# Attention: value products of two chunks in every second step, hash signs by one operation and small transfers

## Chip, cores and metric

One core of one Trainium2 chip runs the whole program. The metric is the device time of one execution in microseconds. The kernel before takes 656.63 us, the median of three runs (654.44 to 657.75).

## What is computed

Three parts follow each other: an attention with hashed masks, and two mixture-of-experts layers. The change lies in the attention, but for one reordering at the end of the last layer. Cut to what matters:

```python
def _attn_ref(q, k, v, proj):              # q, k, v: 2 x 8 heads x 768 x 64, proj: 64 x 6
    q_bits = (einsum('bhsd,dk->bhsk', q, proj) > 0)
    k_bits = (einsum('bhsd,dk->bhsk', k, proj) > 0)
    q_bucket, k_bucket = sum(bits * 2 ** arange(6), axis=-1)     # for each of the two
    mask = q_bucket[:, :, :, None] == k_bucket[:, :, None, :]
    scores = where(mask, scale * q @ k.T, -1e9)
    attn = softmax(scores)                  # with 1e-9 added to the sum
    return attn @ v
```

Two layers follow, `_moe_ref` (routing by capacity, 8 experts of 512 x 1024 x 512) and `_moe2_ref` (a gate per token, one expert per token). All inputs and outputs are float32.

## The kernel before

The attention works on 16 units. A unit `u` is a pair of heads (a = 0, 1) and one half (384 rows) of the queries; it has six steps `i`, each for one head and 128 queries, so 96 steps in all. A step written in the loop of `attention` issues, in this order:

- `score(u, i)`: four matmuls into the PSUM tile S (L191, the product of the rounded parts Q1 and K1, and L193, that of Q2 and K2, each of 512 and 256 columns). Rows 64 to 75 of Q2 and K2 hold the twelve sign rows of the hash, so the mask comes out of L193. VectorE then takes the negated maximum (L195) and two small operations (L196, L197) that give the scale g and the bias b of the exponential. S has two buffers, so the S of a step needs the exponential of two steps before to be done.
- the splits of Q and K for later units (L130, L139, L146), and the loads (L113, L117, L124) on the queue of SyncE (SP), all in program order.
- `av(u', c)`: the product of the transposed probabilities PT with the values, for one of six chunks `c` of 128 keys. One call issues a matmul for each head (L227), each in its own half of the array's columns. Steps 4 and 5 of a unit do chunks 0 and 1 of the unit before, steps 0 to 3 chunks 2 to 5 of the unit before that one.
- `project(...)`: the hash projections of the next unit's queries (step 3), and of keys (step 3, and in some units step 1). Up to four matmuls (L162), each with 64 rows and 12 columns of weights in its own corner of the array, write rows 0 to 11 of the four quarters of one PSUM tile `aux`. VectorE then makes a sign tile of each (L168 for queries, L176 for keys), writing straight to rows 64 to 75 of Q2 or K2. Two of these follow in the step of the projection, the others in the next step.
- `tpose(u', ip, cp)`: four transposes (L213) into one PSUM tile pT (two buffers) and its copy by ScalarE to PT (L216). An even step does two of these groups, an odd step one.
- `expo(u, i)`: the exponential on ScalarE (L204), with the sum of the row. In an even step it lies between the two copies of PT on ScalarE, in an odd step behind the one copy.

At step 0, `fin` (L270) turns a finished unit to rows, and the router's logits come of it. The order on each engine is the order in which the program issues: nothing reorders it. TensorE changes between three ways of being divided: whole (S, transposes, `fin`), two column halves (`av`), and eight corners (`project`).

`splits` and `projs` (set up before the loop) say at which step each split and projection comes; `kplan` says at which unit which key block is split and projected. Units 5 to 8 take two key blocks each; the second is projected at step 1 of the next unit. Keys come through three buffers (`kd`), which are free again when split and projected. `later`, at step 3 of unit 2, issues the constants of the two later layers, among them a chain of small GpSimd operations and three SP transfers behind it (L1103, L1107).

In the last layer, `tile2` computes a tile of 128 tokens; its result `o` (L1441), two small operations on the row index (`ix`, `ixi`, L1444 and L1446) and the scatter by GpSimd (L1454) end it.

Of the kernel before, what the change touches and what calls it, by code (L numbers as in the profile page):

```python
# [7 lines left out]
F32 = mybir.dt.float32  # L8
# [3 lines left out]
I32 = mybir.dt.int32  # L12
AF = mybir.ActivationFunctionType
ALU = mybir.AluOpType
# [4 lines left out]
BIG = 2.0 ** 33  # L19
TINY = 1e-37  # L20
# [3 lines left out]
class Net:  # L24
# [17 lines left out]
    def consts(self):  # L42
        nc = self.nc
# [3 lines left out]
        x = self.x = self.rows.enter_context(self.pool("xp", 1))  # L47
# [8 lines left out]
        ri = x.tile([12, 1], I32, name="ri")  # L56
        nc.gpsimd.iota(ri, pattern=[[0, 1]], base=0, channel_multiplier=1)
        thr = self.thr = x.tile([12, 2], F32, name="thr")
        nc.vector.tensor_scalar(thr[:, 0:1], ri, 5.5, -TINY, op0=ALU.is_gt, op1=ALU.mult)
        nc.vector.tensor_scalar(thr[:, 1:2], ri, 5.5, -TINY, op0=ALU.is_lt, op1=ALU.mult)  # L60

        sg = x.tile([128, 2, 12], F32, name="sg")
# [6 lines left out]
    def signs(self):  # L69

        nc, x = self.nc, self.x
        pr = x.tile([128, 12], F32, name="pr")
        nc.sync.dma_start(pr, self.A["proj"])
        self.prs = x.tile([128, 2, 12], F32, name="prs")
        nc.vector.tensor_tensor(self.prs, self.sg, pr[:, None, :].to_broadcast([128, 2, 12]), op=ALU.mult)
# [17 lines left out]
    def attention(self, r, later):  # L93

        nc, A = self.nc, self.A
        with self.rows as ctx:
# [52 lines left out]
            def project(fs, tag="aux"):  # L149

                p = ps.tile([128, 384], F32, name="aux", tag=tag, bufs=1 if tag == "aux" else 2)
                gs = [f(x, y, p[32 * i:32 * i + 12], i) for i, (f, x, y) in enumerate(fs)]
                for g in gs:
                    next(g)
                for i, g in enumerate(gs):
                    next(g)
                    if i == 1:
                        yield

            def quarter(p, i, which, a):  # L160
                r = 64 * (i % 2)
                nc.tensor.matmul(p, self.prs[r:r + 64, which, :], a[r:r + 64], start=True, stop=True, tile_position=(r, 32 * i))  # L162

            def projq(u, a, p, i):
                d = UD[u]
                quarter(p, i, 0, d["q", a])
                yield
                nc.vector.tensor_scalar(d["Q2", a][64:76], p, self.thr[:, 0:1], None, op0=ALU.is_gt)  # L168
                yield

            def projk(g, j, p, i):
                d = KH[g]
                sl = slice(j * 384, (j + 1) * 384)
                quarter(p, i, 1, d["k"][:, sl])
                yield
                nc.vector.tensor_scalar(d["K2"][64:76, sl], p, self.thr[:, 1:2], -BIG, op0=ALU.is_gt, op1=ALU.mult)  # L176
                yield
# [154 lines left out]
            for _ in project([(projk, 0, 0), (projk, 0, 1), (projq, 0, 0), (projq, 0, 1)]):  # L332
                pass
# [18 lines left out]
            left = None  # L352
            for u in range(NU):
                for i in range(6):
# [14 lines left out]
                    ua, ca = (u - 1, i - 4) if i >= 4 else (u - 2, i + 2)  # L369
                    if ua >= 0:  # L370
                        av(ua, ca)

# [8 lines left out]
                    if (u, i) in projs:  # L381
                        left = project(projs[u, i])
                        next(left, None)
# [682 lines left out]
class Moe:  # L1066
# [330 lines left out]
    def tile2(self, W, rows, x, tick, nxt=None, last=False):  # L1397
# [42 lines left out]
        o = self.m2.tile([128, 512], F32, name="o9") if last else sb.tile([128, 512], F32, name="o2", tag="yr1", bufs=2)  # L1440
        v.scalar_tensor_tensor(o, py, tb[:, 2:3], xr, op0=ALU.mult, op1=ALU.add)  # L1441
# [4 lines left out]
        v.scalar_tensor_tensor(ixi, tb[:, 1:2], -1.0, ix[:, 0:1], op0=ALU.add, op1=ALU.add)  # L1446
        if last:
            return o, ixi
# [276 lines left out]
```

## Time and profile before

| | |
|---|---|
| median of 3 runs | 656.63 us |
| the profiled execution | 658.05 us, span 656.3 us, mean granted clock 0.964 |
| TensorE (PE) | busy 607.8 us, 93% of the span |
| weight loads (PEld) | 423.6 us |
| VectorE (DVE) | 487.2 us, 74% |
| ScalarE (ACT) | 399.7 us, 61% |
| GpSimd (POOL) | 158.1 us |
| HBM read and written | 88.72 and 12.46 MB |

The span is the time from the first to the last instruction of the profiled execution; 1.75 us lie around it. A busy share is an average over the whole program. The attention fills about the first 265 us, the routing of the first layer lies up to about 320 us, and the two layers fill the rest. In the attention PE's busy time is modelled and overlaps itself, so that the starts of its instructions say more than their lengths.

### The profile page before, as it was taken

The page shows a single profiled execution, that of the slowest core. Times are in us where ns is not written, and L with a number is a line of the kernel's source. Part 1 is how long each engine was busy: PE and PEld are TensorE (multiplying, and loading weights), DVE is VectorE, ACT ScalarE, POOL GpSimd, SP SyncE. Part 2 cuts the span into 40 slices and gives each one's busy share as a digit, 9 for nine tenths or more (in the row PEclk, how much of TensorE's full clock was granted, in tenths as well). Part 3 has the DMA queues.
Part 4 walks back from the last instruction along what each step waited for, and adds up shares of the span by engine and source line. Part 5 has one row for each costly group of instructions (what it writes and reads, how often), then busy time and mean ns, then how long its engine had stood idle before and what let it go on. Part 6 is the DMA issues. An engine that isn't in the chain of part 4 may idle for free.

```text
span 656.3 us, 11406 instructions
## 1 busy us (share of the span) xinstructions
PE 607.8 (93%) x3781; PEld 423.6 (65%) x3781; DVE 487.2 (74%) x1542; ACT 399.7 (61%) x909; POOL 158.1 (24%) x212
## 2 busy tenths in 40 slices
PE   6999999999999999865878899999999999999994
PEld 3656665555566656745647486686786778877883
DVE  6888888889786786574848676867643567999991
ACT  5777777776777777412434554554554556887881
POOL 2343233332111110250103031221502322311110
PEclk8899999999999999957989899999999999999998
DMA  6214323312300010053367827558665379999800
GB/s 216 64 60 124 116 76 98 97 38 73 98 25 25 1 50 2 1 201 131 129 188 273 280 39 281 171 176 265 223 218 178 109 278 344 384 379 330 299 14 23
DMA packets 53239, 99.69 MB, mean 152 GB/s; under 512 B 6421, under 2 KB 12949, under 8 KB 53168
## 3 DMA queue, kind: packets, MB, share of 16 engines
q1 hardware_dynamic: 42016, 76.21, 35.0%
q10 hardware_dynamic: 7072, 13.63, 6.0%
q0 software_dynamic: 4080, 8.99, 4.2%
q8 instruction: 34, 0.56, 0.3%
q14 instruction: 37, 0.30, 0.2%
HBM read 88.72 MB, written 12.46 MB: 154 GB/s over the span
## 4 chain that ended last, share of the span: by engine, by line
PE 30%; DVE 10%; issue 6%; DMA 4%; ACT 2%; POOL 1%; POOLq 0%; ACTq 0%; DVEq 0%
PE ph L1166 10%; PE y L1191 6%; PE y L1197 4%; DVE wlo L1353 4%; DMA out<-o,ixi 3%; DMA xg<-xd,idsb 1%; PE pr L1235 1%; PE py L1414 1%; PE py L1413 1%; PE py L1412 1%; PE ph L1412 1%; PE pxt L1145 1%; PE ph L1413 1%; PE ph L1414 1%; ACT whi L1352 1%
## 5 line engine op out<-in xcount | busy, mean ns | idle before, releaser
L1353 DVE TENSOR_TENSOR wlo<-w,whi 128x512 fp32r<-128x512 f32 x192 | 123.6, 685 | 22.6 <-ACT whi L1352 20.8
L216 ACT ACTIVATE PT<-pT 128x512 f32<-128x512 f32 x135 | 79.8, 595 | 52.8 <-PE pT L213 52.1
L195 DVE TENSOR_REDUCE nm<-S 128x1 f32<-128x768 f32 x96 | 91.8, 956 | 25.9 <-PE S L193 24.1
L1352 ACT ACTIVATE whi<-w 128x512 fp32r<-128x512 f32 x192 | 109.4, 622 | 0.4 <-issue 0.4
L1166 PE MATMUL ph<-xT,w 128*128 128x192 f32 x512 | 103.0, 345 | 4.5 <-PEq L1518 4.5
L204 ACT ACTIVATE P<-S,b,g 128x768 f32<-128x768 f32 x96 | 94.7, 987 | 13.3 <-DVE b L197 11.7
L213 PEld LDWEIGHTS pT<-idf,P 128*128 128x128 f32 x576 | 62.4, 142 | 51.4 <-issue 30.7
L1166 PEld LDWEIGHTS ph<-xT,w 128*128 128x128 f32 x512 | 84.1, 195 | 14.9 <-issue 10.2
L213 PE MATMUL pT<-idf,P 128*128 128x128 f32 x576 | 84.7, 282 | 0.7 <-ACT PT L219 0.3
L227 PE MATMUL av<-PT,vd 128*64 128x384 f32 x360 | 77.5, 511 | 0.0
L191 PE MATMUL S<-K,Q 128*128 128x512 f32 x192 | 58.7, 387 | 5.3 <-ACT P L204 4.1
L146 POOL TENSOR_TENSOR Q<-qd,Q 64x384 fp32r<-64x384 f32 x30 | 31.0, 1033 | 134.2 <-PE pT L213 73.1
L1171 ACT ACTIVATE h<-ph 128x128 f32<-128x128 f32 x64 | 17.7, 276 | 60.0 <-PE ph L1166 30.7
L193 PE MATMUL S<-K,Q 76*128 76x512 f32 x192 | 51.0, 347 | 1.8 <-DVE Q L168 1.8
L191 PEld LDWEIGHTS S<-K,Q 128*128 128x128 f32 x192 | 29.7, 194 | 10.6 <-issue 5.8
L193 PEld LDWEIGHTS S<-K,Q 76*128 76x128 f32 x192 | 30.4, 195 | 6.4 <-issue 2.1
L139 POOL TENSOR_TENSOR K<-kd,K 64x768 fp32r<-64x768 f32 x15 | 27.2, 1815 | 26.3 <-DVE K L130 14.5
L1197 PE MATMUL y<-w,h 128*64 128x512 f32 x128 | 33.2, 624 | 0.0
L227 PEld LDWEIGHTS av<-PT,vd 128*64 128x64 f32 x360 | 18.0, 134 | 22.7 <-issue 19.2
L1314 POOL DMA_INDIRECT tb<-rec,ii x16 | 15.9, 996 | 64.7 <-DVE cnt L1311 48.5
L1414 PE MATMUL py<-whi,hl 128*128 128x512 f32 x72 | 29.3, 407 | 1.4 <-DVE hl L1423 1.3
L1412 PE MATMUL py<-whi,hh 128*128 128x512 f32 x72 | 29.9, 415 | 0.0
(374 smaller groups left out, 1100.6 us busy)
## 6 DMA issues: line engine op xcount, KB each, us to landing
w<-w SPq DMA_DIRECT2D x28, 1024.0 KB, 8.5
w<-u SPq DMA_DIRECT2D x26, 1024.0 KB, 9.6
kd<-kT SPq DMA_DIRECT2D x16, 384.0 KB, 4.7
qd<-qT SPq DMA_DIRECT2D x32, 192.0 KB, 3.8
w<-u ACTq DMA_DIRECT2D x6, 1024.0 KB, 13.2
w<-w ACTq DMA_DIRECT2D x4, 1024.0 KB, 7.6
xd<-X SPq DMA_DIRECT2D x4, 780.0 KB, 4.2
vd<-v SPq DMA_DIRECT2D x16, 192.0 KB, 4.0
```

What stands on the lines that cost most here:

```text
L191: nc.tensor.matmul(S[:, n0:n1], d["Q1", a][:, ts], kd["K1"][:, n0:n1], start=True, stop=False)
L193: nc.tensor.matmul(S[:, n0:n1], d["Q2", a][:, ts], kd["K2"][:, n0:n1], start=False, stop=True)
L195: nc.vector.tensor_reduce(d["nm"][:, c], S, op=ALU.max, axis=AX.X, negate=True)
L204: nc.scalar.activation(P, S, AF.Exp, bias=d["b"][:, c], scale=d["g"][:, c], accum_out=d["s"][:, c])
L213: nc.tensor.transpose(p[:, a, b, :], d["P"][2 * ip + b][:, (2 * cp + a) * 128:(2 * cp + a + 1) * 128], self.idf)
L216: nc.scalar.activation(dst, p.rearrange("p a b q -> p a (b q)"), AF.Copy)
L227: nc.tensor.matmul(d["av"][64 * a:64 * a + 64, :], VH[b * 8 + 2 * p + a][:, c, :], d["PT"][:, c, a * 384:(a + 1) * 384], start=(c == 0), s ...
L1166: nc.tensor.matmul(ph, w1[f // 4][:, d, f % 4 * 128:f % 4 * 128 + 128], xT[:, d, :], start=(d == 0), stop=(d == 3))
L1197: nc.tensor.matmul(y2[64 * h:64 * h + 64, :], h2[:, 4 * h + f, :], res["w2"][h][:, f, :], start=(f == 0), stop=(f == 3))
L1352: nc.scalar.activation(hi[:, c, :], w[:, c, :], AF.Copy)
L1353: nc.vector.tensor_tensor(lo[:, c, :], w[:, c, :], hi[:, c, :].bitcast(F32), op=ALU.subtract)
L1412: nc.tensor.matmul(out, a[0][:, i, :], hi[:, i % 4, :], start=start, stop=False)
```

## The change

`av` is called twice in each odd step instead of once in every step: at step 5 for chunks 0 and 1 of the unit before, at steps 1 and 3 for chunks 2, 3 and 4, 5 of the unit before that. `project` gives each projection 32 columns of weights (20 of them zero), with the queries in the quarters 0 and 1 of `aux` and the keys in 2 and 3, and makes the signs of all of them by one VectorE operation (L172) with a threshold and a factor for each partition, into a tile `signs` of one buffer. One SP transfer for each projection then carries 12 x 384 values (18 KB) of it to Q2 or K2. Projection and signs are a step apart now. Only the first two calls, at the start, still write the signs directly (`direct`), by four operations and by two. In `tile2` the index operations come ahead of `o`.

```diff
+            def project(fs, direct=False):
+                p = ps.tile([128, 384], F32, name="aux")
+                qs, ks = [f for f in fs if f[0] is projq], [f for f in fs if f[0] is projk]
+                gs = [(2 * k + i, f(x, y)) for k, l in enumerate((qs, ks)) for i, (f, x, y) in enumerate(l)]
+                for i, (which, a, dst) in gs:
+                    r = 64 * (i % 2)
+                    nc.tensor.matmul(p[32 * i:32 * i + 32, :], self.prs[r:r + 64, which, :], a[r:r + 64], start=True, stop=True,
+                                     tile_position=(r, 32 * i))
+                yield
+                if direct:
+                    for i, (which, a, dst) in gs:
+                        rows = slice(32 * i, 32 * i + 12)
+                        nc.vector.tensor_scalar(dst, p[rows], self.thr[rows, 0:1], self.thr[rows, 1:2], op0=ALU.is_gt, op1=ALU.mult)
+                    return
+                rows = slice(0 if qs else 64, 128 if ks else 64)
+                sg = ld.tile([128, 384], F32, name="signs", bufs=1)
+                nc.vector.tensor_scalar(sg[rows], p[rows], self.thr[rows, 0:1], self.thr[rows, 1:2], op0=ALU.is_gt, op1=ALU.mult)
+                for i, (which, a, dst) in gs:
+                    nc.sync.dma_start(dst.bitcast(F32), sg[32 * i:32 * i + 12, :])
...
-            for _ in project([(projk, 0, 0), (projk, 0, 1), (projq, 0, 0), (projq, 0, 1)]):
+            for _ in project([(projk, 0, 0), (projk, 0, 1), (projq, 0, 0), (projq, 0, 1)], True):
...
-                    ua, ca = (u - 1, i - 4) if i >= 4 else (u - 2, i + 2)
-                    if ua >= 0:
+                    ua, ca = (u - 1, 0) if i == 5 else (u - 2, i + 1)
+                    if i % 2 and ua >= 0:
                         av(ua, ca)
+                        av(ua, ca + 1)
...
-                        left = project(projs[u, i])
+                        left = project(projs[u, i], u == 0 and i == 0)
...
-        o = self.m2.tile([128, 512], F32, name="o9") if last else sb.tile([128, 512], F32, name="o2", tag="yr1", bufs=2)
-        v.scalar_tensor_tensor(o, py, tb[:, 2:3], xr, op0=ALU.mult, op1=ALU.add)
         ix = sb.tile([128, 2], F32, name="ix")
         v.tensor_scalar(ix[:, 0:1], tb[:, 1:2], 0.5, self.trash, op0=ALU.is_lt, op1=ALU.mult)
         ixi = (self.m2 if last else sb).tile([128, 1], I32, name="ixi9" if last else "ixi")
         v.scalar_tensor_tensor(ixi, tb[:, 1:2], -1.0, ix[:, 0:1], op0=ALU.add, op1=ALU.add)
+        o = self.m2.tile([128, 512], F32, name="o9") if last else sb.tile([128, 512], F32, name="o2", tag="yr1", bufs=2)
+        v.scalar_tensor_tensor(o, py, tb[:, 2:3], xr, op0=ALU.mult, op1=ALU.add)
```

The other lines of the diff widen the thresholds `thr` to 128 partitions and the signed projection `prs` to 32 columns, with some ten small VectorE operations at the start.

TensorE in unit 12, steps 4 and 5, before (names: S is written from K and Q, `pT` from the probabilities P and the identity; lines of the kernel before):

```order
L191 MATMUL S<-K_1352,Q_2267 128x512
L191 MATMUL S<-K_1352,Q_2267 128x256
L193 MATMUL S<-K_1353,Q_2268 128x512
L193 MATMUL S<-K_1353,Q_2268 128x256
L227 MATMUL av<-PT,vd 64x384 x2
L213 MATMUL pT<-idf,P 128x128 x8
L191 MATMUL S<-K_1352,Q_2267 128x512
L191 MATMUL S<-K_1352,Q_2267 128x256
L193 MATMUL S<-K_1353,Q_2268 128x512
L193 MATMUL S<-K_1353,Q_2268 128x256
L227 MATMUL av<-PT,vd 64x384 x2
L213 MATMUL pT<-idf,P 128x128 x4
```

The same two steps with the change (lines of the changed kernel: L197 and L199 are the S products, L219 the transposes, L233 the value products):

```order
L197 MATMUL S<-K_1562,Q_2475 128x512
L197 MATMUL S<-K_1562,Q_2475 128x256
L199 MATMUL S<-K_1563,Q_2476 128x512
L199 MATMUL S<-K_1563,Q_2476 128x256
L219 MATMUL pT<-idf,P 128x128 x8
L197 MATMUL S<-K_1562,Q_2475 128x512
L197 MATMUL S<-K_1562,Q_2475 128x256
L199 MATMUL S<-K_1563,Q_2476 128x512
L199 MATMUL S<-K_1563,Q_2476 128x256
L233 MATMUL av<-PT,vd 64x384 x4
L219 MATMUL pT<-idf,P 128x128 x4
```

The value products have left the even step, and stand as four in a row in the odd one.

The queue of SP in unit 2, step 3, and after it, before:

```order
L1076 DMA wsg<-wsg 128x4x9
L1103 DMA tb<-ztab 128x388
L1107 DMA ys<-zrow 128x386 x2
L124 DMA qd<-qT 128x384 x2
L113 DMA kd<-kT 128x768
```

And with the change:

```order
L1084 DMA wsg<-wsg 128x4x9
L1111 DMA tb<-ztab 128x388
L1115 DMA ys<-zrow 128x386 x2
L174 DMA Q_494<-signs 12x384
L174 DMA Q_521<-signs 12x384
L174 DMA K_554<-signs 12x384 x2
L129 DMA qd<-qT 128x384 x2
L118 DMA kd<-kT 128x768
```

The sign transfers for unit 3 (Q_494 is its Q2 of head 0) stand behind the three transfers of the constants.

The same queue in unit 6 with the change, from its loads at step 1 to the signs of step 4:

```order
L129 DMA qd<-qT 128x384 x2
L118 DMA kd<-kT 128x768
L122 DMA vd<-v 128x384
L118 DMA kd<-kT 128x768
L122 DMA vd<-v 128x384
L174 DMA K_1205<-signs 12x384 x2
L174 DMA Q_1293<-signs 12x384
L174 DMA Q_1329<-signs 12x384
L174 DMA K_1369<-signs 12x384 x2
```

The loads stood there in this order before, with nothing between them and the next unit's. The key signs that step 1 projected (K_1205) are now behind the second load of keys, and the query signs for unit 7 behind both.

## Rows read from the trace of the kernel before

**Rows 1.** Windows of 10 us: stretch, length, then each engine's busy time, clock, DMA.

```profile
80.00:90.00 10.00, 10.00 (x64) 6.39 (x62) 8.89 (x22) 7.41 (x16) 2.39 (x4) 1.00 0.26 78
```

**Rows 2.** Groups by line, 0 to 340 us: busy us, mean ns, idle before.

```profile
L176 DVE TENSOR_SCALAR K<-aux,thr 12x384 fp32r<-12x384 f32 x32 | 19.7, 615 | 0.7
L168 DVE TENSOR_SCALAR Q<-aux,thr 12x384 fp32r<-12x384 f32 x32 | 19.5, 610 | 1.1
```

**Rows 3.** Timeline of PE, unit 7 from step 4: start, length, instruction.

```profile
125.88 0.60 PE L191 MATMUL S<-K,Q 128*128 128x512 f32 x2
126.31 0.52 PE L193 MATMUL S<-K,Q 76*128 76x512 f32 x2
...
127.56 1.09 PE L213 MATMUL pT<-idf,P 128*128 128x128 f32 x8
128.41 0.59 PE L191 MATMUL S<-K,Q 128*128 128x512 f32 x2
...
130.07 0.66 PE L213 MATMUL pT<-idf,P 128*128 128x128 f32 x4
130.49 0.59 PE L191 MATMUL S<-K,Q 128*128 128x512 f32 x2
...
133.73 0.61 PE L191 MATMUL S<-K,Q 128*128 128x512 f32 x2
```

**Rows 4.** Timeline of PE in unit 0, a step without value products.

```profile
22.47 0.51 PE L193 MATMUL S<-K,Q 76*128 76x512 f32 x2
22.82 0.60 PE L213 MATMUL pT<-idf,P 128*128 128x128 f32 x4
```

**Rows 5.** Timeline of PE behind the loop: three chunks in a row.

```profile
263.09 2.16 PE L227 MATMUL av<-PT,vd 128*64 128x384 f32 x12
265.08 0.50 PE L312 MATMUL S<-PT,vd 128*64 128x128 f32 x6
```

**Rows 6.** Timeline of ACT in unit 7, step 3 (its last two operations).

```profile
126.16 0.60 ACT L216 ACTIVATE PT<-pT 128x512 f32<-128x512 f32 x1 [0.84 <-PE pT L213]
126.65 0.99 ACT L204 ACTIVATE P<-S,b,g 128x768 f32<-128x768 f32 x1
```

**Rows 7.** Timeline of all engines, unit 1, step 1: S waits for an exponential.

```profile
25.10 0.99 ACT L204 ACTIVATE P<-S,b,g 128x768 f32<-128x768 f32 x1 [0.66 <-DVE b L197]
...
26.23 0.62 PE L191 MATMUL S<-K,Q 128*128 128x512 f32 x2 [0.80 <-ACT P L204]
```

**Rows 8.** Timeline of DVE in unit 8, step 0.

```profile
131.53 0.95 DVE L195 TENSOR_REDUCE nm<-S 128x1 f32<-128x768 f32 x1
...
132.70 0.16 DVE L197 TENSOR_TENSOR b<-g,nm 128x1 f32<-128x1 f32 x1
```

**Rows 9.** Timeline of SP in unit 7: the second keys and what follows.

```profile
125.63 0.33 SPq L113 DMA_DIRECT2D kd<-kT  x1
...
127.14 0.91 SPq L124 DMA_DIRECT2D qd<-qT  x2
```

**Rows 10.** DMA issues: count, KB each, median us from issue to landing.

```profile
ys<-zrow SPq DMA_DIRECT2D x2, 193.0 KB, 3.7
...
tb<-tb SPq DMA_DIRECT2D x10, 2.0 KB, 1.9
```

**Rows 11.** Timeline of SP: the constants' last two transfers.

```profile
52.20 0.92 SPq L1107 DMA_DIRECT2D ys<-zrow  x2
```

**Rows 12.** Timeline of PE at the start of unit 3: its first L193.

```profile
52.75 0.51 PE L193 MATMUL S<-K,Q 76*128 76x512 f32 x2
```

**Rows 13.** Timeline of all engines at the start: the first wait for signs.

```profile
9.89 0.59 PE L193 MATMUL S<-K,Q 76*128 76x512 f32 x2 [1.77 <-DVE Q L168]
```

**Rows 14.** Timeline of PE at the end of unit 9.

```profile
164.41 0.59 PE L191 MATMUL S<-K,Q 128*128 128x512 f32 x2 [0.84 <-ACT P L204]
```

**Rows 15.** Timeline of DVE at the end of the program.

```profile
647.56 0.75 DVE L1441 SCALAR_TENSOR_TENSOR o<-py,tb,xr 128x512 f32<-128x512 f32 x1 [2.87 <-PE py L1414]
...
648.46 0.16 DVE L1446 SCALAR_TENSOR_TENSOR ixi<-tb,ix 128x1 int32<-128x1 f32 x1
```

More of the change, by code (lines that the diff above doesn't have):

```diff
@@ L54, in consts @@
         nc.gpsimd.iota(jp, pattern=[[1, 128]], base=0, channel_multiplier=-1)
-        ri = x.tile([12, 1], I32, name="ri")
+        ri = x.tile([32, 1], I32, name="ri")
         nc.gpsimd.iota(ri, pattern=[[0, 1]], base=0, channel_multiplier=1)
[L58 to L62, printed above, removed]
+        thr = self.thr = x.tile([128, 2], F32, name="thr")
+        for i in range(4):
+            nc.vector.tensor_scalar(thr[32 * i:32 * i + 32, 0:1], ri, 5.5, -TINY, op0=ALU.is_gt if i < 2 else ALU.is_lt, op1=ALU.mult)
+        nc.vector.memset(thr[0:64, 1:2], 1.0)
+        nc.vector.memset(thr[64:128, 1:2], -BIG)
+        sg = x.tile([128, 2, 32], F32, name="sg")
+        nc.vector.memset(sg, 0.0)
         nc.vector.memset(sg[:, 0, 0:6], 1.0)
@@ L73, in signs @@
         nc.sync.dma_start(pr, self.A["proj"])
-        self.prs = x.tile([128, 2, 12], F32, name="prs")
-        nc.vector.tensor_tensor(self.prs, self.sg, pr[:, None, :].to_broadcast([128, 2, 12]), op=ALU.mult)
+        self.prs = x.tile([128, 2, 32], F32, name="prs")
+        nc.vector.tensor_copy(self.prs, self.sg)
+        nc.vector.tensor_tensor(self.prs[:, :, 0:12], self.sg[:, :, 0:12], pr[:, None, :].to_broadcast([128, 2, 12]), op=ALU.mult)
     def ident(self):
@@ L147, in splitq @@
                 copy(ceng, Q2[0:64], d["q", a][0:64])
[L149 to L162, printed above, removed]
@@ L164, in projq @@
-            def projq(u, a, p, i):
-                d = UD[u]
[L166 to L171, printed above, removed]
+            def project(fs, direct=False):
[17 more added lines that the diff above has]
+                    nc.sync.dma_start(dst.bitcast(F32), sg[32 * i:32 * i + 12, :])
@@ L172, in projk, with projq @@
+            def projq(u, a):
+                d = UD[u]
+                return 0, d["q", a], d["Q2", a][64:76]
+            def projk(g, j):
                 d = KH[g]
                 sl = slice(j * 384, (j + 1) * 384)
[L174 to L177, printed above, removed]
+                return 1, d["k"][:, sl], d["K2"][64:76, sl]
             def score(u, i):
```

## Prediction

> **What bounds the kernel now.** I looked first at windows of the attention: in 80 to 90 us PE is busy for all of 10 us, DVE for 8.89, ACT for 7.41 [rows 1]. Busy PE says little, so I went to the timeline of PE, by starts. Unit 7, step 4, begins at 125.88, step 5 at 128.41, unit 8 at 130.49 and its step 1 at 133.73 [rows 3]: an even step takes 2.53 us, an odd one 2.08, and step 0 with the finished unit's matmuls 3.24. PE waits for nobody there. So the order of work on PE sets the pace, and DVE, from which the change takes most, is not late in the middle units. The other engines matter by the moment at which they give PE its next tile; I took those from the timelines of ACT, DVE and SP.
>
> **The value products.** The second part of S to the transposes is 1.25 us with one chunk between (126.31 to 127.56) [rows 3], and 0.35 without (22.47 to 22.82) [rows 4]; four transposes take 0.66 behind a chunk and 0.60 behind S [rows 3, 4]. One visit to the column halves costs 0.90 + 0.06, say 0.95 us. Three chunks in a row take 263.09 to 265.08, 0.66 each [rows 5]. Putting two visits together so saves 0.95 - 0.66 = 0.29 us of PE. The even step falls from 2.53 to 1.58, the odd one rises from 2.08 to 2.74; a pair from 4.61 to 4.32.
>
> But the shorter even step runs into ACT. S of the next odd step needs the exponential of the last one. In an odd step ACT copies the transposes first: the copy starts at 126.16, 0.28 behind the start of the next S (125.88), and the exponential 0.49 later [rows 3, 6]. Where S has waited for an exponential, it started 1.13 behind that one's start (25.10 to 26.23) [rows 7]. So from the start of the even step's S to the odd step's S there are at least 0.28 + 0.49 + 1.13 = 1.90 us, against 1.58 of PE's own work. Today 2.53 covers it. The pair becomes 1.90 + 2.74 = 4.64: 0.03 longer than 4.61. Only the pair with step 0 keeps its gain: its even step falls from 3.24 to 2.29, still above 1.90.
>
> 13 pairs of that kind (units 3 to 15): -3.8 us. 28 others: +0.8; if the chain did not bind, -8.1; I allow +2.8 (0.1 each) for a release that is later than the one shown.
>
> **The signs.** The 64 sign operations take 0.61 us each [rows 2]; six stay (`direct`), 58 become 19 of the same 384 columns (one at step 4 of units 0 to 14, one at step 2 of units 6 to 9). I take 0.61 for one on 128 partitions, since rows changed and columns did not. That is 39 x 0.61 = 24 us of DVE, worth only what DVE holds up (below). In exchange the query signs go by transfer. Their path, from the start of S at step 4: S ends 0.95 later (126.31 + 0.52 - 125.88) [rows 3]; maximum to bias 1.33 (131.53 to 132.86) [rows 8]; with 0.07 between, the sign operation starts at 2.35 and ends at 2.96; I allow 0.1 to the issue on SP. No row shows an 18 KB transfer inside the chip. The nearest in size, of 2 KB, lands 1.9 behind its issue, and 193 KB takes 3.7 [rows 10]. I take 1.9, for it is nearest: 4.96, and 0.05 for PE to start. PE needs them in L193 of the next unit: 1.90 + 2.74 + 0.43 = 5.07 behind the same start. They come 0.06 early, so 0 us; the cover is that thin. With 0.4 more on the landing each of 12 units would wait some 0.4: up to +5. Before, DVE wrote these signs one step earlier, and no transfer followed.
>
> **Unit 3.** The signs for it stand on SP behind the constants' chain. SP issued the last of those transfers by 53.12 [rows 11]; GpSimd's chain ahead of it is not changed. The first sign transfer is issued at 53.2 and lands at 55.1 at the earliest. Behind 193 KB that land at 3.7 from an issue at 52.7, it would be 56.4. PE wants them at 52.75 [rows 12], and by the new step times within 0.1 of that. PE waits 2.4 to 3.7; I take +3.1. The Trainium skill, DMA: Bandwidth & Descriptors, section Queues, rings and completion order, says that each of the DMA engines takes its descriptors in ring order, but that completion is not first in, first out for an issuing engine; a short transfer on few rings could so land before the large one, which speaks for 2.4 and would make the sum 0.7 less. No row here shows two such transfers.
>
> **Units 7 and 8.** In units 6 and 7 the key signs of step 1 stand behind the second load of keys, which waits for the projection of step 3 (issued at 125.63 in unit 7) [rows 9]. SP reached the next issue at 127.14, and two issues there took 0.91, so both key transfers are issued by 128.0 and the last (issued at 127.6) lands at 129.5; 0.7 earlier, if the load of values between would be issued as fast as that of keys (0.33), and 0.8 later, if the transfers wait for the loads ahead of them. `signs` has one buffer: the sign operation of step 4, ready at 125.88 + 2.35 = 128.23, waits for them. Behind it on DVE are the next maximum and exponential's bias, which have time, and behind it on SP are the query signs. PE has them at 129.6 + 0.61 + 0.1 + 1.95 = 132.3 and wants them at 125.88 + 5.07 = 130.95: it waits 1.3 (0.6 to 2.1). Twice: +2.6. In unit 9 no loads of keys follow, in unit 8 the one load is free at step 1.
>
> **Start, router's units, end.** At the start PE waits for the third of four sign operations [rows 13]; keys now come last, so it waits for the fourth: +0.6. Units 0 to 2 are not paced by PE: DVE loses nine sign operations there (5.5 us), of which I count 0.4 us, because the signs of unit 1 now wait for a landing too: +0.2 together (-3 to +1.9). In units 9, 10 and 14, which also count for the router, DVE is late: 0.84 of idle PE at 164.41 [rows 14]. In unit 9 six sign operations become two: -0.8 (0 to -2). At the end the two index operations leave the path: 648.62 - 648.31 = 0.31 [rows 15], -0.3. In the tiles before, DVE works on weight parts without a break, so nothing else. Twenty zero columns of weights change no streamed column: 0. The some ten small operations at the start I count at 0, since PE's first wait is for the splits and signs behind the loads [rows 13]; uncovered they would be below 1 us.
>
> **Sum.** -3.8 + 0.8 + 0 + 3.1 + 2.6 + 0.2 - 0.8 - 0.3 = +1.8 us. Against the profiled execution's 658.05 that is 659.85; it lies 1.42 above the median of 656.63, so the median becomes 658.4. A measurement of this kernel can tell 0.5% (3.3 us) from no change: 653.35 and 659.9 are the bounds.
>
> **Rivals.**
> - Every unit waits for its signs. Place: L193 at step 0. It decides from a landing over 1.95 us; with the 2.4 of a somewhat larger or more disturbed transfer each of 12 units pays 0.45: +5.4, 663.8. For it: the margin of 0.06, and that the loads share the queue. Against: at step 4 the loads of step 1 have landed.
> - The exponential does not bind. ACT is busy for 7.41 of 10 us [rows 1], so its copy and exponential could come earlier than I chain them. Then 28 pairs give -8.1 instead of +0.8: 649.5. Against: ACT's copy stood right behind its transposes, with ACT idle ahead of it for 0.84 [rows 6]; there is nothing to bring forward.
> - The special waits (unit 3, units 7 and 8) are hidden, because PE comes later or SP earlier than I reckon: -5.7, 652.7. Against: both follow from the order on SP, not from durations near each other.
>
> **Chances.** Forecast 0.45 (its own range 655.5 to 661.5), late signs everywhere 0.31, free exponential 0.16, hidden waits 0.08. Faster: most of the last two, 0.20. Slower: the late signs and the forecast's upper tail, 0.36. Within 0.5%: 0.44. The range of 651 to 664.5 leaves out most of the free exponential and of late signs with over 0.5 us each.
>
> **What would show it.** In the changed profile: pairs of steps 2 to 5 at 4.6 us with PE waiting some 0.3 for the exponential in every odd step; step 0 with 2.3; a wait for a transfer in the first L193 of unit 3 of 2.4 to 3.7 us and of units 7 and 8 of about 1.3, and none above 0.2 elsewhere; the sign operation waiting on DVE at step 4 of units 6 and 7. Wrong it would be, if pairs took 4.3, or if every unit's start showed a wait.

## The result and the profile after

The changed kernel took 665.79 us (663.92 to 667.89) where the kernel before took 656.59 beside it; the ratio is 1.0145, with a 95% interval of 1.0096 to 1.0195. A second set (below) gave 665.50 and 1.0140 [1.0107, 1.0173]. So it is slower by about 9 us (9.2 in the first set, 8.6 in the second), where I had forecast 1.8 us and a range up to 664.5. One more execution of 839.85 us, with a mean clock of 0.647, is left out.

The profiled execution of after took 663.92, 5.87 more than the profiled one of before: their spans are 662.15 and 656.28. I cut both by the start of the first scores (S0), of each unit's first scores and of the last matmul into the tile `vl` (L292 before, L298 after), all read from PE's timeline. Beside it stands what my terms give for the same stage:

| stage | before us | after us | difference | forecast |
|---|---|---|---|---|
| ahead of S0, units 0 to 2 | 52.31 | 51.85 | -0.46 | +0.20 |
| unit 3 | 15.33 | 18.08 | +2.75 | +2.87 |
| units 4 to 6 | 46.75 | 46.80 | +0.05 | -0.69 |
| units 7 and 8 | 32.18 | 34.87 | +2.69 | +2.14 |
| units 9 to 14 | 97.27 | 96.55 | -0.72 | -2.18 |
| unit 15 to the last matmul into `vl` | 35.36 | 36.67 | +1.31 | -0.23 |
| the rest | 377.08 | 377.34 | +0.26 | -0.30 |
| sum | 656.28 | 662.15 | +5.87 | +1.81 |

The big terms are there, at nearly their size. PE's timeline in unit 5 shows the pairs (start, length; in brackets the idle time ahead and who ended it):

```profile
90.47 0.60 PE L197 MATMUL S<-K,Q 128*128 128x512 f32 x2
90.90 0.51 PE L199 MATMUL S<-K,Q 76*128 76x512 f32 x2
91.25 1.04 PE L219 MATMUL pT<-idf,P 128*128 128x128 f32 x8
92.46 0.59 PE L197 MATMUL S<-K,Q 128*128 128x512 f32 x2 [0.17 <-ACT P L210]
92.89 0.52 PE L199 MATMUL S<-K,Q 76*128 76x512 f32 x2
93.34 1.51 PE L233 MATMUL av<-PT,vd 128*64 128x384 f32 x8
...
95.97 0.60 PE L197 MATMUL S<-K,Q 128*128 128x512 f32 x2
...
97.88 0.62 PE L197 MATMUL S<-K,Q 128*128 128x512 f32 x2
...
100.64 0.60 PE L197 MATMUL S<-K,Q 128*128 128x512 f32 x2
```

Step 2 takes 1.99 (90.47 to 92.46) and ends in a wait for the exponential; step 4 takes 1.91, step 5 2.76. That is the chain on ACT that I drew from [rows 3, 6, 7]; with before's 2.53 and 2.08 nothing is won in these pairs.

SP and PE at the start of unit 3, to be read beside [rows 11, 12]:

```profile
51.55 0.92 SPq L1115 DMA_DIRECT2D ys<-zrow  x2
52.57 1.64 SPq L174 DMA_DIRECT2D Q<-signs  x2
54.27 1.48 SPq L174 DMA_DIRECT2D K<-signs  x2
```

```profile
51.85 0.60 PE L197 MATMUL S<-K,Q 128*128 128x512 f32 x2
55.08 0.59 PE L199 MATMUL S<-K,Q 76*128 76x512 f32 x2 [2.63 <-DMA Q<-signs]
```

The signs leave SP right behind the constants' last transfer, and PE, which has done the first half of its scores, stands for 2.63 us until they are there, 2.51 after their issue began. Windows of the same stretch (the last two figures are the DMA engines' busy share and GB/s) show that no byte moved from 53.75 to 54.00, between the constants and the 18 KB of the first sign transfer:

```profile
53.75:54.00 0.25, 0.00 (x0) 0.00 (x0) 0.00 (x0) 0.00 (x0) 0.00 (x0) 1.00 0.00 0
54.00:54.40 0.40, 0.00 (x0) 0.00 (x0) 0.00 (x0) 0.00 (x0) 0.00 (x0) 1.00 0.22 46
```

In units 6 and 7 the one buffer of signs holds the sign operation, as forecast. DVE and SP in unit 6, then PE at the start of unit 7:

```profile
114.23 0.16 DVE L203 TENSOR_TENSOR b<-g,nm 128x1 f32<-128x1 f32 x1
115.66 0.68 DVE L172 TENSOR_SCALAR signs<-aux,thr 128x384 f32<-128x384 f32 x1 [1.27 <-DMA K<-signs]
```

```profile
112.72 1.53 SPq L174 DMA_DIRECT2D K<-signs  x2
116.36 1.48 SPq L174 DMA_DIRECT2D Q<-signs  x2
```

```profile
116.73 0.60 PE L197 MATMUL S<-K,Q 128*128 128x512 f32 x2
118.41 0.62 PE L199 MATMUL S<-K,Q 76*128 76x512 f32 x2 [1.08 <-DMA Q<-signs]
```

What I had not forecast is a wait for signs ahead of unit 15. DVE in unit 14, SP, then PE:

```profile
245.74 0.82 DVE L588 TENSOR_SCALAR gn<-mrow,m 128x1152 bf16<-128x1152 f32 x1
246.47 0.74 DVE L588 TENSOR_SCALAR go<-mrow,m 128x384 bf16<-128x384 f32 x2
247.13 0.67 DVE L172 TENSOR_SCALAR signs<-aux,thr 64x384 f32<-64x384 f32 x1
```

```profile
247.88 1.60 SPq L174 DMA_DIRECT2D Q<-signs  x2
```

```profile
248.14 0.60 PE L197 MATMUL S<-K,Q 128*128 128x512 f32 x2
249.95 0.62 PE L199 MATMUL S<-K,Q 76*128 76x512 f32 x2 [1.20 <-DMA Q<-signs]
```

The sign operation stands behind three operations for the router, so its signs leave 1.4 us later than in the units before. And the durations of the new instructions, from the views by tile and by line (min, median, max in ns; the last line is of the operations that still write the keys' signs straight, on 12 partitions):

```profile
L174 SPq DMA_DIRECT2D Q<-signs x30: 714/731/924, 22.9 to 248.8; - x30
L174 SPq DMA_DIRECT2D K<-signs x28: 713/714/762, 24.6 to 170.2; - x28
L172 DVE TENSOR_SCALAR signs<-aux,thr x19: 667/677/689, 22.2 to 247.1; 128x384 f32<-128x384 f32 x10, 64x384 f32<-64x384 f32 x9
L168 DVE TENSOR_SCALAR K<-aux,thr x4: 674/680/687, 8.8 to 14.7; 12x384 fp32r<-12x384 f32 x4
```

A second thing not forecast lies in unit 9, a unit that also counts for the router. DVE there, then PE:

```profile
160.37 1.81 DVE L559 TENSOR_TENSOR baq<-baq,rW 128x24 f32<-128x24 f32 x1
...
162.64 0.69 DVE L172 TENSOR_SCALAR signs<-aux,thr 64x384 f32<-64x384 f32 x1
```

```profile
163.38 0.51 PE L162 MATMUL aux<-qd,prs 64*32 64x384 f32 x2 [0.85 <-DVE signs L172]
```

The sign operation of step 1's projection is now issued in step 2, behind the router's operations, and `aux` has one buffer: PE's next projection waits 0.85 us until the signs have been read out of it.

The table explains 5.9 us, the medians differ by about 9. The profiled execution of after was the fastest of its set, that of before (658.05) lay above its three. The rest is looked for with the experiments.

### The profile page after: what moved, and what is told of

Its sections match the earlier page's. It is cut to its first block, busy times and chain, and to the rows that moved or that the text cites. A ratio compares the mean times of both kernels' runs of the same rounds, so it can differ in the third digit from the quotient of the medians.

```text
span 662.1 us, 11507 instructions
## 1 busy us (share of the span) xinstructions
PE 604.7 (91%) x3781; PEld 432.7 (65%) x3781; DVE 464.8 (70%) x1509; ACT 400.2 (60%) x909; POOL 159.1 (24%) x212
## 4 chain that ended last, share of the span: by engine, by line
PE 29%; DVE 10%; issue 6%; DMA 4%; ACT 2%; POOL 1%; POOLq 0%; DVEq 0%; ACTq 0%
PE ph L1174 10%; PE y L1199 6%; DVE wlo L1361 4%; PE y L1205 4%; DMA out<-o,ixi 3%; DMA xg<-xd,idsb 1%; PE pr L1243 1%; PE py L1422 1%; PE py L1421 1%; PE pxt L1153 1%; PE py L1420 1%; ACT whi L1360 1%; PE ph L1420 1%; PE ph L1421 1%; PE ph L1422 1%
## 5 line engine op out<-in xcount | busy, mean ns | idle before, releaser
L1174 PE MATMUL ph<-xT,w 128*128 128x192 f32 x512 | 104.6, 348 | 3.9 <-PEq L1526 3.9
L219 PEld LDWEIGHTS pT<-idf,P 128*128 128x128 f32 x576 | 64.9, 142 | 30.2 <-ACT PT L222 11.4
L219 PE MATMUL pT<-idf,P 128*128 128x128 f32 x576 | 82.8, 279 | 2.0 <-ACT mrow L577 1.7
L233 PE MATMUL av<-PT,vd 128*64 128x384 f32 x360 | 68.0, 499 | 0.0
L197 PE MATMUL S<-K,Q 128*128 128x512 f32 x192 | 59.2, 390 | 5.6 <-ACT P L210 4.1
L199 PE MATMUL S<-K,Q 76*128 76x512 f32 x192 | 51.8, 351 | 10.0 <-DMA Q<-signs 7.1
L199 PEld LDWEIGHTS S<-K,Q 76*128 76x128 f32 x192 | 30.1, 193 | 17.2 <-issue 6.8
L197 PEld LDWEIGHTS S<-K,Q 128*128 128x128 f32 x192 | 29.8, 195 | 15.4 <-ACT P L210 9.6
L233 PEld LDWEIGHTS av<-PT,vd 128*64 128x64 f32 x360 | 21.8, 136 | 27.3 <-issue 27.3
```

Of the source, the lines that this page charges most:

```text
L197: nc.tensor.matmul(S[:, n0:n1], d["Q1", a][:, ts], kd["K1"][:, n0:n1], start=True, stop=False)
L199: nc.tensor.matmul(S[:, n0:n1], d["Q2", a][:, ts], kd["K2"][:, n0:n1], start=False, stop=True)
L219: nc.tensor.transpose(p[:, a, b, :], d["P"][2 * ip + b][:, (2 * cp + a) * 128:(2 * cp + a + 1) * 128], self.idf)
L233: nc.tensor.matmul(d["av"][64 * a:64 * a + 64, :], VH[b * 8 + 2 * p + a][:, c, :], d["PT"][:, c, a * 384:(a + 1) * 384], start=(c == 0), s ...
L1174: nc.tensor.matmul(ph, w1[f // 4][:, d, f % 4 * 128:f % 4 * 128 + 128], xT[:, d, :], start=(d == 0), stop=(d == 3))
```

## The experiments

Each was timed in five rounds beside the kernel before, in four sets (median of before in them: 656.43, 656.92, 656.68 and 657.12).

**The pairs alone** (the kernel before with this one edit):

```
-ua, ca = (u - 1, i - 4) if i >= 4 else (u - 2, i + 2)
-if ua >= 0:
+ua, ca = (u - 1, 0) if i == 5 else (u - 2, i + 1)
+if i % 2 and ua >= 0:
     av(ua, ca)
+    av(ua, ca + 1)
```

> The kernel before with the value products in pairs and nothing else; all signs are written by VectorE as before. My theory, with step times read from the changed kernel: an odd step's S waits for the exponential, so pairs of steps take 4.66 to 4.7 us as before and only the pair with step 0 gains 0.29. Units 4 to 6 and 11 at 15.1 us, no wait for a transfer anywhere, 654 to 657 us. Rival one, the pairing itself costs the time: 663 to 667. Rival two, the pairing gives 0.29 in every pair and the signs eat it: 644 to 647, units at 14.5.

656.21 us, ratio 0.9993 [0.9974, 1.0011]. Units 3 to 5 take 15.20 instead of 15.33. So this half of the change costs nothing and brings nothing that can be measured. In its profile units 3 to 14 take 189.54 us together, 1.99 less than before, and the median is only 0.2 lower; what took the rest back is weighed at the end of the next section.

**The signs alone** (the changed kernel with the value products in every step again, the edit above turned back):

> The changed kernel with the value products back in every step; signs by one operation and transfers stay. My theory: the waits for signs stay at the first L199 of unit 3 (about 2.8 us), units 7 and 8 (1.3 each), unit 15 (about 1) and at the start (0.8), DVE gives 1 to 2 back in units 9, 10 and 14: 660 to 663 us. Rival, the pairing costs the time and the signs nothing: 655 to 658, and no such waits.

668.75, ratio 1.0188 [1.0156, 1.0220]: the whole loss, and 6 us above the range that was expected. Step 0 of unit 3 took 9.06 us, with a wait of 3.0 and a granted clock of 0.50 for 6.8 us from 57.9 on; step 0 of units 7 and 8 took 4.61 and 5.17 against 3.24, of units 4 to 6 3.41 to 3.46.

**The constants one place later** (changed kernel, their chain at step 5 of unit 2):

```
-(2, 3): later
+(2, 5): later
```

> The changed kernel with the constants of the later layers issued at step 5 of unit 2 instead of step 3, so that the sign transfers for unit 3 stand ahead of them on SP. My theory: step 0 of unit 3 falls from 5.17 us to about 2.4, the time by 2.7 against the changed kernel: 661 to 665. Rival, the wait of unit 3 comes from the landing and not from the place in the queue: step 0 still over 4.5, 664 to 668.

660.84, ratio 1.0068 [1.0042, 1.0093]: a little better than expected. Unit 3 fell from 18.08 to 15.39, 2.7 us; the median fell by 4.7 to 5. Taking away a wait of 2.6 us won nearly twice that. Between the two profiled executions the gain is only 1.8 (663.92 and 662.11), mostly because the part ahead of unit 3 took 53.31 in this one and 51.85 in the other.

**Key signs of step 1 written straight** (changed kernel; no transfer for them, so the buffer is free):

```
-left = project(projs[u, i], u == 0 and i == 0)
+left = project(projs[u, i], u == 0 and i == 0 or i == 1)
```

> The changed kernel with the key signs that step 1 projects (units 6 to 9) written straight by VectorE, two operations each, no transfer. My theory: the sign operation of step 4 in units 6 and 7 no longer waits for the one buffer, step 0 of units 7 and 8 falls from 3.65 and 3.87 us to about 2.4, 2.7 us less than the changed kernel: 661 to 665. Rival, the query signs are late there because SP itself is busy with loads and transfers: step 0 stays above 3.3.

664.20, ratio 1.0119 [1.0097, 1.0142], inside the expected range; by the time alone it cannot be told from the changed kernel (1.0140 [1.0107, 1.0173]). Step 0 of units 7 and 8 came from 3.65 and 3.87 to 2.48 and 2.47: the one buffer was the cause. The profiled execution lost it again in unit 4, where step 0 took 4.87 with a wait of 1.91 put down to the signs, and the clock fell behind it. The signs were not late there: SP issued them at 69.89, as early in the unit as in the changed kernel, and the first transfer's bytes had moved by 71.6, 2.4 us before PE went on. What held PE is not shown.

**The sign operation one step earlier** (changed kernel; step 3's signs in step 3):

```
 left = project(projs[u, i], u == 0 and i == 0)
 next(left, None)
+if i == 3:
+    next(left, None)
+    left = None
```

> The changed kernel with the sign operation of step 3's projection issued in step 3 instead of step 4, nothing else mended. It is about unit 15, whose query signs leave late because the sign operation of step 4 in unit 14 stands behind VectorE's operations for the router (wait of 1.2 us in the changed kernel). Theory 1: the wait ahead of unit 15 goes (step 0 of 3.75 us comes to 2.5), units 4 to 6 lose their 0.1 us, units 3, 7 and 8 keep their waits (3: 2.7 us, 7 and 8: 1.3), since constants and key signs stand ahead on the same queue: 1.5 to 2.5 us under the changed kernel, 663 to 664.5. Theory 2 (a sign operation that comes earlier and still waits for the buffer of signs in units 6 and 7 now holds the maximum behind it): units 6 and 7 lose 0.5 to 1 us each, and the time stays at 664.5 to 667.

666.90, ratio 1.0163 [1.0125, 1.0200]. Step 0 of unit 15 came from 3.78 to 2.31 and units 4 and 5 from 15.34 and 15.37 to 15.22: both as theory 1 has it. Units 6 and 7 lost 2.1 and 2.7, theory 2 at more than twice its price, and the time is in the range of theory 2. DVE there:

```profile
116.45 0.68 DVE L172 TENSOR_SCALAR signs<-aux,thr 128x384 f32<-128x384 f32 x1 [3.50 <-DMA K<-signs]
117.05 0.95 DVE L201 TENSOR_REDUCE nm<-S 128x1 f32<-128x768 f32 x1
...
118.30 0.95 DVE L201 TENSOR_REDUCE nm<-S 128x1 f32<-128x768 f32 x1
```

The operation that waits for the buffer now has two maxima queued behind it, and PE stands for 1.99 us.

**All three mends together:**

> The changed kernel with three mends: the router's constants loaded at step (2, 5) instead of (2, 3); the key signs projected in step 1 written straight into K2 as before; the sign operation of step 3's projection issued in the same step, so that the query signs leave a step earlier. Theory 1 (the added time is waits for signs and what follows from them): no wait of TensorE for a transfer of signs is left in units 3 to 15, units 3, 7 and 8 have their lengths of before to 0.2 us, and the time is that of before to 2 us, 654 to 659. Theory 2 (one operation for four sign rows, or its transfers, cost time of themselves, beside the waits): 660 to 664 with no wait in the trace. By either, nothing is gained against the pairs alone (656.2), since VectorE does not set the length of a step.

655.40, ratio 0.9986 [0.9966, 1.0006]: theory 1. PE waits for no transfer of signs from unit 3 on; units 3 to 5 take 15.22, 7 and 8 15.99. PE at the start of unit 3:

```profile
53.22 0.60 PE L197 MATMUL S<-K,Q 128*128 128x512 f32 x2
53.66 0.52 PE L199 MATMUL S<-K,Q 76*128 76x512 f32 x2
```

So taking away the waits for signs, with what follows from them, takes the whole loss away: 10 us between the two kernels. The wait for `aux` in unit 9 is still there, now of 1.52 us. Whether the constants' later place does anything for the kernel before by itself was not tried; its PE waits for nothing at that place [rows 12]. The 20 us of DVE time that this kernel saves (467.4 busy for 487.2 before) are worth nothing measurable as long as DVE does not set a step.

**Keys' signs first at the start** (mended kernel, `gs[len(qs):] + gs[:len(qs)]` in the direct branch):

> The mended kernel (constants at (2, 5), step 1's key signs written straight, step 3's sign operation in its own step), and at the start the four direct sign operations in the order of before: the two of the keys ahead of the two of the queries. It is about the start alone. Theory 1 (the keys' signs coming last hold the first scores): the wait of TensorE ahead of its first half with signs falls from 2.6 us to 1.8, unit 0 is 0.7 to 1 us shorter, the time 0.5 to 1.5 us under the mended kernel's 655.4 (0.9986 of before): 0.996 to 0.998 of before. Theory 2 (what is lost at the start is the granted clock, which comes back half later): the wait shortens and the time stays, 0.998 to 1.0 of before.

655.59, ratio 0.9979 [0.9959, 0.9998]. The wait fell from 2.84 to 2.27, unit 0 from 18.98 to 17.72, and the median did not move: nearer to theory 2, though 1 us cannot be told here.

**PE kept busy in unit 3's wait** (changed kernel):

```
+if (u, i) == (3, 0):
+    self.awake(ps.tile([128, 384], F32, name="aux")[:, 0:256], 24)
```

> The changed kernel with 24 idle products of 256 columns put on TensorE into the wait of unit 3, between the first and the second half of its first scores, so that TensorE is busy while it waits for the signs. The wait itself stays. Theory 1 (the idle wait lets the granted clock fall behind it in some executions, as in 57.9 to 64.7 us of the kernel with signs alone, and this is what the wait costs above its own 2.7 us): unit 3 stays at 17.9 to 18.4 us, no stretch of 1.2 GHz between 55 and 85 us, and the median is 1.5 to 3 us under that of the changed kernel in this same set, 663 to 665. Theory 2 (the clock after the wait has nothing to do with it): the same as the changed kernel to 1 us, or slower by the products that run past the wait's end.

**The changed kernel again**, beside it:

> The changed kernel itself once more, beside the three above on the same chip. By every theory 664 to 668 (1.0145 of the time before, as in its first measurement). If stretches at 1.2 GHz after unit 3's wait are what spreads its times, this profile shows one between 55 and 85 us or the first one did not by chance.

665.42 with the idle products, 665.50 without, the latter as expected. The profile of the one shows no stretch of 1.2 GHz between 55 and 85 us, that of the other does. Here are its windows (stretch, length, busy time of PE, PEld, DVE, ACT, POOL, granted clock, DMA) and PE's timeline:

```profile
54.40:57.60 3.20, 0.59 (x5) 0.27 (x2) 0.00 (x0) 1.57 (x3) 0.00 (x0) 1.00 0.57 197
57.70:61.10 3.40, 3.38 (x14) 3.30 (x15) 1.80 (x5) 1.51 (x3) 0.52 (x1) 0.50 0.47 136
61.20:64.00 2.80, 2.80 (x19) 1.55 (x18) 2.32 (x7) 0.54 (x2) 0.61 (x2) 1.00 0.55 193
```

```profile
57.72 0.98 PE L199 MATMUL S<-K,Q 76*128 76x512 f32 x2 [2.73 <-DMA Q<-signs]
58.50 1.91 PE L219 MATMUL pT<-idf,P 128*128 128x128 f32 x8
```

PE stood for 2.73 us, and from the moment it went on it had half its clock for 3.4 us: L219 took 1.91 instead of 1.04, and unit 3 19.80 instead of 18.08. But the median is the same with the idle products, so my theory that they would save 1.5 to 3 us fell. Whether they kept the clock up, or that one execution was lucky, six runs of each do not tell.

The two profiled executions of the changed kernel are 4.7 us apart (668.65 and 663.92), and nearly all of it lies in two places: the part ahead of unit 3 (54.39 against 51.85 us) and unit 3. Both spend more time at 1.2 GHz in the slower execution; over the first 30 us the mean granted clock is 0.72 there and 0.83 in the faster one, as in the kernel before. The clock's record is not complete, though. With the idle products it shows 1.00 for the first 30 us, while L197 there took 1.01 us instead of 0.60:

```profile
0.00:30.00 30.00, 24.31 (x94) 14.97 (x95) 18.66 (x50) 16.51 (x31) 6.11 (x10) 1.00 0.38 122
```

```profile
8.35 1.01 PE L197 MATMUL S<-K,Q 128*128 128x512 f32 x2
```

**The exponential first** (pairs alone; in odd steps ACT's exponential ahead of its copy, six buffers of P):

```
+if gp < 0 or g % 2:
+    expo(u, i)
 if gp >= 0:
 ...
-if gp < 0 or g % 2:
-    expo(u, i)
```

> The kernel before with the values' products in pairs (signs as before), and in the odd steps the exponential is issued ahead of the transposes' copy instead of behind it (a sixth buffer for P goes with it). Theory 1: what sets the length of a pair of steps, 4.65 us in units 3 to 5 with pairs, is the chain scores, maximum, exponential, release of S, so that the copy ahead of the exponential in ScalarE's queue is on the path of the odd step; without it a pair takes 4.2 to 4.4 us, a unit 14.3 to 14.7 instead of 15.2, and the time falls by 5 to 9 us to 647 to 652. Theory 2: TensorE's own work fills the pair, so the order on ScalarE does not matter: within 2 us of the pairs alone, 654 to 658. Theory 3: the copy that now comes late holds the values' products, and it is slower: 658 to 662.

666.40, ratio 1.0159 [1.0128, 1.0190], outside all three. Units 11 and 13, without keys to sign, fell to 14.75, as theory 1 has it; units 3 to 10 rose to 15.98 up to 19.19, nearly all of it in step 0. DVE and PE in unit 5:

```profile
85.11 1.25 DVE L176 TENSOR_SCALAR K<-aux,thr 12x384 fp32r<-12x384 f32 x2
86.39 0.96 DVE L195 TENSOR_REDUCE nm<-S 128x1 f32<-128x768 f32 x1
```

```profile
87.18 0.60 PE L213 MATMUL pT<-idf,P 128*128 128x128 f32 x4
89.47 0.66 PE L213 MATMUL pT<-idf,P 128*128 128x128 f32 x4 [1.69 <-ACT PT L216]
```

Two sign operations, 1.25 us together, stand ahead of step 5's maximum. The exponential waits for it at the head of ACT's queue, the copy behind the exponential, and PE for the copy. Here DVE's sign operations do set the pace, and the change's one operation for all should help.

**The exponential first with the mended signs:**

> The kernel of the run beside this one (mended signs, keys first at the start), with the exponential of the odd steps issued ahead of the transposes' copy as in e5_pairs_exp_first (six buffers of P; a values' buffer and two small ones less make room). In e5 the units without key signs (11 and 13: 14.75 us against 15.2) gained and those with them (3 to 10) lost 0.8 to 1.8 us in step 0: there two sign operations of the keys, 1.24 us, stand in VectorE's queue between the maxima of steps 4 and 5, and the exponential that now leads ScalarE's queue waits for the second maximum. Theory 1: the sign operation for all rows takes this work away from that place, so all units come to 14.7 to 14.8 (with a second projection 15.3 to 15.6): 0.45 us times 12 units, about 5 us less than the run beside it, 649 to 651 (0.988 to 0.992 of before). Theory 2 (it is not VectorE's sign operations that made step 0 late in units 3 to 10, but loads or splits of the keys): those units stay at 16 to 17, slower than before by 1% or more, 662 to 668.

657.53, ratio 1.0011 [0.9989, 1.0033]. Units 3 to 5 and 11 and 13 came to 14.8, so theory 1 holds for the cause there; the time lies between what the two theories gave. Units 6 to 8, with two key blocks to sign, rose from 15.99 to 16.43, unit 9 (router) from 18.32 to 19.68, unit 1 from 12.60 to 15.02: the gain was given back.

**The exponential first only where it won** (units 2 to 5 and 10 to 14):

```
+early = u in (2, 3, 4, 5, 10, 11, 12, 13, 14)
-if gp < 0 or g % 2:
+if gp < 0 or g % 2 and early:
     expo(u, i)
```

> The mended kernel with keys first at the start, and the exponential ahead of the copy in the odd steps of units 2 to 5 and 10 to 14 alone, where the run before gained (14.8 us against 15.2); units 0, 1, 6 to 9 and 15, where it lost (16.4 against 16.0, 19.7 against 18.3, 15.0 against 12.6), keep the order of before. Theory 1 (the gains and losses belong to their units): 0.4 us in each of units 3 to 5 and 11 to 14, 0.7 in units 2 and 10: unit 15 starts about 4 us earlier after the first scores than in the kernel with keys first (235.5 us), at 231 to 232, and the time is 650 to 653, 0.990 to 0.995 of before. Theory 2 (TensorE packed more densely is granted 1.2 GHz for longer, as the mean clocks of the runs suggest: about 46 us of it in the kernel before, 49 with pairs, 52 in the run with the exponential first): the units come out as in theory 1, but half of the gain or more is not in the time: 653 to 656.

652.59, ratio 0.9935 [0.9911, 0.9958], theory 1: the one version that is faster than both kernels, by 4 us, with its whole interval below 1. From S0 to unit 15 it takes 231.5 us, the kernel before 236.3. PE in unit 4:

```profile
77.51 0.60 PE L197 MATMUL S<-K,Q 128*128 128x512 f32 x2
...
79.09 0.60 PE L197 MATMUL S<-K,Q 128*128 128x512 f32 x2
...
81.83 0.60 PE L197 MATMUL S<-K,Q 128*128 128x512 f32 x2
```

The pair is 1.58 + 2.74 = 4.32, the very numbers I had worked out for pairs without the chain on ACT. In units 11 and 13 the order on ACT gave this with the signs of before as well (14.75); units 3 to 5 came to 15.98 to 16.54 with those and to 14.8 with the mended ones.

## Why the prediction was wrong

The direction was right, but +1.8 was less than the 3.3 us that the prediction itself counted as a change, and the size was wrong: +5.9 in the profiled pair, about +9 in the medians. Two terms failed outright, the 0 us for the query signs and the -0.8 for the router's units; the pairs brought 2.0 instead of 3.0; and some 3 us by which the medians differ beyond the profiled pair were in no term.

- **Pairs.** Right: "0.03 longer than 4.61". Measured +0.05 in steps 4 and 5, +0.13 in steps 2 and 3, -0.30 with step 0, so -0.13 in a unit instead of -0.23. With pairs alone units 3 to 14 won 1.99 and unit 15 nothing (35.36 both times), where 3.0 was forecast for the thirteen. The release in step 2 is 0.10 later than the one I had chained. The first kernel of the experiments has the time of before; the last one shows that the chain named is the one that binds.
- **Unit 3.** Right in place and size: 2.63 of wait in the range of 2.4 to 3.7, +2.75 for the unit. I took 3.1 and gave 2.4 by the rule in the Trainium skill (DMA: Bandwidth & Descriptors, Queues, rings and completion order); the trace lies nearer to that. That rule lets a short transfer finish ahead of a large one issued before it. Here none had to: the constants' bytes had all moved before the first sign byte did, so the 2.4 came near without that rule. Wrong was the worth of the wait: taking it away gave 4.7 to 5 us.
- **Units 7 and 8.** Right: step 0 is 3.65 and 3.87 where 2.29 + 1.3 was forecast, DVE's wait for the buffer is in the trace, and straight writing took it away.
- **"They come 0.06 early, so 0 us; the cover is that thin."** This is the step that failed first. The sign operation took 0.07 longer than I had taken (0.68 for 0.61), and from issue to use it was 2.07 instead of 1.95 (unit 15): with the 0.06 taken off, 0.13 late. The 0.07 did not come with the rows: with the factor read from a tile, an operation on 12 partitions took 0.68 too. The units with the signs a step earlier take 15.22, those of after 15.34 and 15.37, and that is the 0.13. Ahead of unit 15 I had not looked at what stands in front of the sign operation on DVE in a router's unit: 1.2 us of wait. Units 4 to 6 and 15 are 2.3 us of the 4.1 that the profiled sum missed, 0.5 of it from the pairs.
- **Router's units.** Failed: "-0.8" for DVE's relief in units 9, 10 and 14. The six units 9 to 14 gained 0.72 instead of 2.18, and with pairs alone unit 9 was even shorter (17.15 against 17.65). The 0.84 of idle PE [rows 14] did go, but the later sign operation cost PE 0.85 for `aux` in the same unit. I had counted the operations that DVE is spared and not where the one that is left stands.
- **Rivals.** "Every unit waits for its signs" named the right mechanism with the wrong place: not 0.45 in each of 12 units, but 0.1 in some and 1.2 in one. Its 663.8 was the nearest number, by luck: the 5.4 us in 12 units are not there.
- **Start.** +0.2 was forecast. The part ahead of unit 3 was 0.46 shorter than before in one profiled execution and 2.1 longer in the other (52.31 before), so the term cannot be judged by one profile.
- **What was in no term: the granted clock.** A span and its mean clock c give the time at 1.2 GHz as 2 x (1 - c) x span. Over all timed runs that is 45 to 48 us for the kernel before (means of its four sets of 17 to 22 runs), 51 and 53 for the changed one (3 and 6 runs), 45 with the constants later, 49 with all mends and with pairs alone. The 45 rests on two of six executions with a mean of 0.975, which may have a gap in the record like the one above; the other four give 51. If a stretch costs half its length, as the 3.4 us in unit 3 that cost 1.72, then 6 us more of it are 3 us, and the rest, 9 - 3 = 6, is about the 5.9 of the table. This fits, as do the stretches right behind waits, the two profiles of the changed kernel and the 2 us of the pairs that the time does not show. But it is argued and not shown: the run that was to show it changed nothing, and the record has gaps. What lengthens these stretches stays open.

## What to carry to other kernels

When work is moved from an engine's write to a transfer, follow it in every kind of unit, not in the middle one: what stands ahead of the operation on its engine, ahead of the transfer on its queue, who holds its buffer, and who waits for the buffer that it holds itself. A cover of 0.06 us worked out from medians is no cover, and should be priced at the next longer duration. Freeing an engine that does not set the pace is worth nothing by itself; look for the order that can use it, here the exponential ahead of the copy, and apply it only in the units where the freed engine leaves room.

## What the runs showed of the hardware

- Seven times in the attention, in six profiled executions, the granted clock was 0.50 (1.2 GHz) for 3.4 to 6.8 us, beginning within 1.6 us of the moment at which TensorE went on after a wait: after 2.73 us at 57.7 (above), after 3.0 with the signs alone (57.9, 0.9 before PE went on), after 1.91 with step 1 written straight (75.6), after 2.00 with pairs and the exponential first (176.8), after 1.94 in unit 9 with the exponential first and mended signs (160.7), and twice with the sign operation one step earlier, of which the first is:

```profile
119.70 0.87 PE L197 MATMUL S<-K,Q 128*128 128x512 f32 x2 [1.99 <-ACT P L210]
120.36 0.84 PE L199 MATMUL S<-K,Q 76*128 76x512 f32 x2
```

```profile
115.50:119.70 4.20, 2.21 (x15) 0.94 (x13) 3.03 (x7) 1.23 (x3) 0.00 (x0) 1.00 0.06 14
119.90:123.10 3.20, 3.20 (x14) 3.01 (x14) 1.79 (x5) 2.60 (x6) 0.10 (x1) 0.50 0.45 134
```

  The wait of 2.63 in unit 3 of the profiled execution of after had no such stretch behind it, nor had the one of 2.68 with the sign operation one step earlier, so a wait of that length is followed by it in some executions and not in others. The Trainium skill (TensorE: Matmul & The Clock Gate, Part 1: The HAM clock gate) says that the lower level is the default and activity of the array releases the higher one; the seven stretches agree, and what decides between a wait with and without one no run here shows.
- A transfer of 18 KB inside the chip kept SP's sequencer for 0.71 to 0.73 us (medians), a load of 192 KB for 0.46 [rows 9]: the smaller transfer is the dearer one to issue. From issue to use it took 2.07 us (unit 15), and 2.51 behind two of 193 KB; in the second case its bytes moved 1.4 us after the issue began, and PE went on 1.1 us later.
- A TENSOR_SCALAR from PSUM with 384 columns took 0.67 to 0.69 us with threshold and factor read from a tile, on 12, 64 and 128 partitions alike. With the threshold alone read from the tile it took 0.61 on 12 [rows 2]. So the partitions cost nothing here; the second value read from a tile is what differs between the two.
